# Batch 0's second softmax turned in 32x32 squares on VectorE, first group first, and the router's matrix in four column tiles

## The chip, the cores and the metric

The kernel runs on one core of one Trainium2 chip. The metric is the device time of one execution in microseconds (us). Before the change it is 726.91 us, the median of three runs (722.82 to 727.24). The engines are TensorE (PE in the rows; its weight loads are PEld), VectorE (DVE), ScalarE (ACT), GpSimd (POOL) and SyncE (SP), and each works through its own queue in order.

## The reference, cut to what matters

There are 8 batches, 8 heads, 576 positions, head dimension 64, 32 packing vectors per head, and a model width of 512.

```python
def sm_attn(qq, kk, vv):                       # softmax of scale * q k^T, times v
    ...
p_packed = sm_attn(p, k, v)                    # first softmax: 32 x 576 per head
out = sm_attn(q, p_packed, p_packed)           # second softmax: 576 x 32 per head
...
gate_pre += conv_w[k] * xp[:, k:k + S, :]      # causal convolution, 5 taps
gate = 1.0 / (1.0 + np.exp(-gate_pre))
val = x @ w_val
x2 = gate * val @ w_out
...
logits = x2 @ w_gate ; local_gate = sigmoid(x2 @ w_local)   # chooses an expert per position
out[b, s] = p[e] * (np.maximum(x2[b, s] @ w1[e], 0.0) @ w2[e])
```

The weights w_val, conv_w and w_out are stored as 64-bit floats and converted on the chip.

## The kernel before

For each batch the kernel computes, in this order: scores of packing vectors against keys (`s1`), first softmax (`softmax1`), its transposes (`a1T`), packed values `pp` (`a1v`), their transpose ppT, scores of queries against them (`s2`, tile s2k), second softmax, the packed values times w_val (`mval`, tile mv), attention output with the convolution (tile xT), `val` times the gate, `logits` and `route`, and the product with w_out (`x2`). Then `expert` runs the two layers of the expert that the first position chose; this is the bulk of the work. Heads are held in two groups g of four heads; the convolution's result has four blocks m of 128 channels, two in each group.

A planner (`Plan.run`) writes out every engine's order before the launch. Each task has an estimated duration, the tasks that must precede it, and tiles in numbered slots. At each step the planner takes the engine that can start first, and of its tasks that can start within 30 ns of the first one, the task with the lowest rank. A rank is the due time, counted back from the expert's goals, plus `later`. The conversion of w_out has `later` 30000. `behind` lets a task start only after another one has started. The estimate for `a1v` is 40 * STEPV + 250 ns. Only the order is kept: on the chip an engine waits for whatever its next instruction needs. PSUM has three slots of two banks for everything but the expert (tag p) and two single banks for the expert (tag f).

Around the change, batch 0 differs from the later batches. Its second softmax (`softmax2_0`, L447) copies the scores to SBUF, turns them on TensorE (L456), runs the softmax on VectorE over both groups (L467 to L477), and turns them back on TensorE (`a2T`, L518). The later batches (`softmax2`, L479) turn them in 32x32 squares on VectorE (L491 and L503), without TensorE. For the convolution, batch 0 forms on TensorE the five taps spread out as matrices (`taps`, L581), multiplies them into `pp` on VectorE (L593, L596), and then does five shifted products for each output block on TensorE (`conv0`, L610). The later batches do one product (`xT`, L552), scale the last tap on ScalarE (L560), add the other four on VectorE straight from PSUM (L564), and take the tanh on ScalarE (L567). The products of batch 0 are in 32-bit floats; each gives two records in the trace. The later ones split their operands into a high and a low half (`split`, L309: the high half on ScalarE, L312, the low one on VectorE, L316) and take three products (`mm3`, L298).

`router` (L666) computes w_out times the router's weights g9 (512 x 9): it turns w_out on TensorE (L677), copies it (L681), and takes 16 products with w_out stationary and 9 moving columns (L688). `logits` (L705) uses the result ww, and `x2` (L656) follows. `setup` loads the weights and converts them (`from_f64`, L897). The loads of the setup come from the SP queue, apart from some small ones; the loads of later batches come from the POOL queue.

Of the kernel before, what the change touches and what calls it, by code (L numbers as in the profile page):

```python
# [13 lines left out]
ALU = mybir.AluOpType  # L14
# [164 lines left out]

PERIOD, MARGIN, SLACK, START, DMA = 87000, 1e6, 1200, 75000, 3500  # L180
EARLY, LATE = 30, 30000
STEP8, STEPV = 30, 27
A2F = 1
TAPS, WARM, RATE, S1B = 'a1v', True, 415.0, [(0, 'xT', 1)]
LASTX = 30000
NPF, NPP, NPS = 2, 3, 0
ACC, WLO, F64 = 4, "POOL", "DVE DVE"
# [4 lines left out]
def packed_attention_gated_conv_moe(  # L192
# [238 lines left out]
    def s2(b):  # L431

        t, qt = st[b, "ppT"], [st[b, "q", j] for j in range(2)]
        pk = [pst([128, 2, 512], f"s2k_{b}_{g}") for g in range(2)]

        def prod():
            for hf in range(2):
                for i, g in heads():
                    n = slice(i % 2 * S + hf * HS, i % 2 * S + hf * HS + HS)
                    nc.tensor.matmul(pk[g][col(i), hf, 0:HS], t[row(g), col(i)], qt[i // 2][row(g), n],  # L440
                                     start=True, stop=True)

        st[b, "s2"] = pe(STEP8 * 32 + 250, prod, r=[t, *qt], w=pk, behind=done((b - 1, "a2T")))
        for g in range(2):
            (softmax2 if b else softmax2_0)(b, g, pk[g])

    def softmax2_0(b, g, pk):  # L447

        sT = ref(big, [128, 640], F32, f"a2l{g}", f"s2t_{g}", 1)
        act(S, lambda: cp(two(sT[:, 0:S]), halves(pk), AF.Copy), ps=True, r=[pk], w=[(sT, 0)])  # L450
        dve(64, lambda: nc.vector.memset(sT[:, S:], 0.0), w=[(sT, 1)])
        ps = pst([128, 8, 128], f"s2_{b}_{g}")

        def turn():
            for c in range(NT):
                nc.tensor.transpose(ps[:, c, :], sT[:, c * 128:c * 128 + 128], ident)  # L456

        pe(5 * 109, turn, r=[sT, f["ident"]], w=[ps])
        r = ref(sm, [128, 3, 20], F32, "s2r", f"s2r_{b}_{g}", 2)
# [7 lines left out]
        dve(640, lambda: nc.vector.tensor_reduce(r[:, 0, :], pv(), AX.X, ALU.max), r=[ps], w=[r])  # L467
        dve(640, lambda: tt(av(), pv(), bc(0), ALU.subtract), r=[ps, r], w=[a2])
        act(640, lambda: cp(a2[:], a2[:], AF.Exp, scale=0.125), r=[a2], w=[a2])
        dve(640, lambda: nc.vector.tensor_reduce(r[:, 1, :], av(), AX.X, ALU.add), r=[a2], w=[r])  # L470
# [5 lines left out]
        dve(280, end, sb=2, r=[r], w=[r])  # L476
        dve(700, lambda: tt(av(), av(), bc(2), ALU.mult), sb=2, r=[a2, r], w=[a2])  # L477

    def softmax2(b, g, pk):  # L479


        nj = S // NP
        a2 = ref(wk, [128, NT * 128], F32, "a2", f"a2_{b}_{g}", 2)
        a2f = st[b, "a2T", g] = ref(wk, [128, S], F32, "a2f", f"a2f_{b}_{g}", A2F)
        r = ref(sm, [128, 3, 20], F32, "s2r", f"s2r_{b}_{g}", 2)
        av = lambda: a2.t[:, 0:S].rearrange("p (j k) -> p j k", k=NP)

        def bc(i):
            return r[:, i, 0:nj].unsqueeze(2).to_broadcast([128, nj, NP])

        dve(S, lambda: nc.vector.transpose(two(a2[:, 0:S]), halves(pk)), r=[pk], w=[a2])  # L491
        dve(S, lambda: nc.vector.tensor_reduce(r[:, 0, 0:nj], av(), AX.X, ALU.max), r=[a2], w=[r])
        dve(S, lambda: tt(av(), av(), bc(0), ALU.subtract), sb=2, r=[r], w=[a2])
        act(S, lambda: cp(a2[:, 0:S], a2[:, 0:S], AF.Exp, scale=0.125), r=[a2], w=[a2])
        dve(S, lambda: nc.vector.tensor_reduce(r[:, 1, 0:nj], av(), AX.X, ALU.add), r=[a2], w=[r])
# [5 lines left out]
        dve(280, end, sb=2, r=[r], w=[r])  # L501
        dve(S, lambda: tt(av(), av(), bc(2), ALU.mult), sb=2, r=[r], w=[a2])
        dve(S, lambda: nc.vector.transpose(a2f[:], a2[:, 0:S]), r=[a2], w=[a2f])  # L503

    def a2T(b, g):
        if b:
            t = st[b, "a2T", g]
            hi = ref(big, [128, S], F32R, f"a2h{g}", f"a2h{g}_{b}", 1)
            lo = ref(big, [128, S], F32R, f"a2l{g}", f"a2l{g}_{b}", 1)
            split(S, lambda: hi[:], lambda: lo[:], lambda: t[:], [t], [hi, lo])  # L510
            st[b, "a2T", g] = (hi, lo)
            return
        a2 = st[b, "a2", g]
        ps = pst([128, 1024], f"a2Tp_{b}_{g}")

# [20 lines left out]
    def xT(b, g):  # L536


        pp, a2 = st[b, "pp", g][b > 0:], st[b, "a2T", g]
        terms = [(0, 0), (0, 1), (1, 0)] if b else [(0, 0)]  # L540
        pss_ = [pst([128, 1024], f"xT_{b}_{2 * g + i}") for i in range(2)]

        def x(i):
            return pss_[i][:, 512 - HS:512 + HS]

        def prod():
            for hf in range(2):
                n = slice(hf * HS, hf * HS + HS)
                for t, (wi, xi) in enumerate(terms):
                    for i in range(2):  # L550
                        m = slice(i * 64, i * 64 + 64)
                        nc.tensor.matmul(x(i)[:, n], pp[wi][m, :], a2[xi][m, n],  # L552
                                         start=(t == 0), stop=(t == len(terms) - 1))

        st["xT"] = st[b, "xT", g] = pe(mm(6) + 200 if b else 1500, prod, r=[*pp, *a2], w=pss_,
                                       behind=done((b - 1, "val"), "val0") if g == 0 else done((b, "val")))
        for i in range(2):
            j, ps = 2 * g + i, pss_[i]
            acc = st[b, "t", j] = ref(wk, [128, S], F32, "acc", f"acc_{b}_{j}", ACC)
            act(S + 100, lambda i=i, j=j, acc=acc: cp(acc[:], x(i), AF.Copy, scale=cw[:, j, KC - 1:KC]),  # L560
                ps=True, r=[ps, f["cw"]], w=[acc])
            for k in range(KC - 1):
                d = KC - 1 - k
                dve(S + 60, lambda i=i, j=j, k=k, d=d, acc=acc: stt(  # L564
                    acc[:, d:], x(i)[:, 0:S - d], cw[:, j, k:k + 1], acc[:, d:], ALU.mult, ALU.add),
                    r=[ps], w=[acc])
            act(S, lambda acc=acc: cp(acc[:], acc[:], AF.Tanh, scale=0.5), r=[acc], w=[acc])  # L567

    def taps():
# [5 lines left out]
            return ps[:, c * 128:c * 128 + 128]  # L575

        def prod():
            for g in range(2):
                for k in range(KC):
                    for i in range(2):  # L580
                        nc.tensor.matmul(place(g, k)[i * 64:i * 64 + 64],  # L581
                                         cw[:, 2 * g + i, k:k + 1].to_broadcast([128, 64]), ident,
                                         start=True, stop=True)

        pe(40 * 60, prod, r=[f["cw"], f["ident"]], w=st["taps"], behind=done(TAPS))

    def conv0(g):

# [77 lines left out]
    def router():  # L666
# [3 lines left out]
        for h in range(2):  # L670
            ps = pst([128, 1024], f"woT{h}")

            def turn(h=h, ps=ps):
# [6 lines left out]
            pe(8 * 109, turn, r=[wo, f["ident"]], w=[ps])  # L680
            act(1024, lambda h=h, ps=ps: cp(woT[:, h * 1024:h * 1024 + 1024], ps[:], AF.Copy), ps=True,  # L681
                r=[ps], w=[(woT, h)])
        ps = pst([128, 1024], "wwp")

        def prod():
# [234 lines left out]
    def setup():  # L920
# [4 lines left out]
        v64 = ref(big, [128, 8 * S], I32, "hh", "val64", 1)  # L925
        o64 = ref(big, [128, 8 * S], I32, "hl", "out64", 1)
        g9 = st["g9"] = ref(sm, [128, 4, 9], F32, "g9", "g9", 1)

        def half(t, src, k):
            q = nc.sync  # L930
# [5 lines left out]
        for x in SETUP.split():  # L936
# [10 lines left out]
            elif x[0] == "w":  # L947
                half(v64 if x[1] == "v" else o64, w_val if x[1] == "v" else w_out, int(x[2]))
            else:
                load(0, x[0], int(x[1]) if x[1:] else 0, nc.sync)  # L950

        def flat(t, k):
            return t.rearrange("p k c -> p (k c)")[:, k * CH:(k + 1) * CH]
# [25 lines left out]
    def attention(b):  # L979
# [9 lines left out]
            a1v(b, g)  # L989
        ppT(b)  # L990
        mval(b)
        if not b:
            taps()
        for g in range(2):
            if b:
                load(b, "q", g, nc.gpsimd)
        s2(b)
        for g in range(2):
            a2T(b, g)
        for g in range(2):  # L1000
            if b:
# [164 lines left out]
```

## Time and profile before

| what | before |
|---|---|
| median of three runs | 726.91 us |
| the profiled execution | 727.72 us |
| its span, first to last instruction | 726.0 us |
| mean granted TensorE clock | 0.977 of 2.4 GHz |
| TensorE busy | 687.0 us, 95% of the span |
| VectorE busy | 430.7 us, 59% |
| ScalarE busy | 289.8 us, 40% |
| GpSimd busy | 236.1 us, 33% |

The span lies inside the execution's own time; the difference of 1.7 us is before the first and after the last instruction. Busy time says how much work an engine has, not where it is waited for. The chain of waits says that: it follows the last instruction back through whatever released it. A "x40" behind a piece counts records.

### The profile page before, as it was taken

What the parts mean: (1) busy time and instruction counts of PE and PEld (TensorE: products, weight loads), DVE (VectorE), ACT (ScalarE), POOL (GpSimd) and SP (SyncE); (2) the same over time, 40 slices, a digit from 0 to 9 for tenths busy, and PEclk for the clock granted to TensorE, in tenths of its full rate; (3) what the DMA queues carried; (4) which work ended last, traced back from release to release, by engine and by line L of the source; (5) the groups of instructions that cost most, each with busy time, mean ns of one, the idle gap of its engine ahead of it and who ended that gap; (6) DMA issues with size and microseconds to landing.
All of it is one profiled execution on the core that took longest, in us unless ns stands there. A gap on an engine that the chain in (4) does not pass through costs nothing.

```text
span 726.0 us, 15236 instructions
## 1 busy us (share of the span) xinstructions
PE 687.0 (95%) x6124; PEld 640.6 (88%) x6124; DVE 430.7 (59%) x874; ACT 289.8 (40%) x565; POOL 236.1 (33%) x250
## 2 busy tenths in 40 slices
PE   3589999999899989999999999999999999999996
PEld 2367989997899879899989989999999999999996
DVE  5972358845884697958688578627972663221311
ACT  3533345433552346444446245424353333312420
POOL 2020344224320623413353044412342144325441
PEclk9877999999899999999999999999999999999999
DMA  8601394228421943715482356314242335243322
GB/s 348 242 1 32 127 330 143 77 85 266 171 60 48 310 153 120 233 49 184 150 257 80 131 183 222 90 45 176 82 134 74 131 97 153 83 165 127 111 89 67
DMA packets 35293, 102.10 MB, mean 141 GB/s; under 512 B 4283, under 2 KB 6899, under 8 KB 32659
## 3 DMA queue, kind: packets, MB, share of 16 engines
q0 software_dynamic: 13616, 56.87, 22.3%
q1 hardware_dynamic: 21314, 44.00, 19.6%
q8 instruction: 50, 0.82, 0.5%
q10 hardware_dynamic: 288, 0.21, 0.1%
q14 instruction: 25, 0.20, 0.1%
HBM read 74.90 MB, written 28.52 MB: 142 GB/s over the span
## 4 chain that ended last, share of the span: by engine, by line
PE 81%; DMA 8%; DVE 4%; issue 3%; POOL 1%; ACT 1%; SPq 0%; POOLq 0%; DVEq 0%; ACTq 0%
PE g L299 17%; PE g L301 16%; PE g L300 15%; DMA codes<-rk 5%; PE x L299 5%; PE x L300 5%; PE x L301 5%; PE val L299 2%; PE val L300 2%; PE val L301 2%; DMA out<-in_w_out_dram 2%; PE xT L552 2%; PE xT L610 2%; PE lg L705 1%; DVE codes L815 1%
## 5 line engine op out<-in xcount | busy, mean ns | idle before, releaser
L314 POOL TENSOR_TENSOR wlo<-raw,whi 128x512 fp32r<-128x512 f32 x128 | 166.4, 1301 | 281.3 <-ACT whi L312 279.0
L299 PE MATMUL g<-x2h,whi 128*128 128x288 f32 x512 | 154.5, 302 | 3.9 <-DVE hl L866 3.8
L299 PE MATMUL g<-hh,whi 128*128 128x288 f32 x512 | 154.2, 301 | 0.4 <-ACT whi L312 0.4
L301 PE MATMUL g<-hh,wlo 128*128 128x288 f32 x512 | 150.9, 295 | 0.9 <-POOL wlo L314 0.9
L301 PE MATMUL g<-x2h,wlo 128*128 128x288 f32 x512 | 151.5, 296 | 0.0
L300 PE MATMUL g<-x2l,whi 128*128 128x288 f32 x512 | 151.5, 296 | 0.0
L300 PE MATMUL g<-hl,whi 128*128 128x288 f32 x512 | 150.7, 294 | 0.0
L312 ACT ACTIVATE whi<-raw 128x512 fp32r<-128x512 f32 x128 | 80.2, 627 | 95.3 <-PE g L300 55.1
L299 PEld LDWEIGHTS g<-x2h,whi 128*128 128x128 f32 x512 | 96.7, 189 | 10.2 <-DVE hl L866 5.3
L299 PEld LDWEIGHTS g<-hh,whi 128*128 128x128 f32 x512 | 96.1, 188 | 7.0 <-issue 5.7
L866 DVE SCALAR_TENSOR_TENSOR hl<-g,hh 128x288 fp32r<-128x288 f32 x128 | 57.7, 453 | 74.9 <-ACT hh L864 74.1
L864 ACT ACTIVATE hh<-g 128x288 fp32r<-128x288 f32 x128 | 52.5, 410 | 114.0 <-PE g L301 113.2
L301 PEld LDWEIGHTS g<-hh,wlo 128*128 128x128 f32 x512 | 96.0, 188 | 1.1 <-POOL wlo L314 1.1
L300 PEld LDWEIGHTS g<-x2l,whi 128*128 128x128 f32 x512 | 96.8, 189 | 0.0
L301 PEld LDWEIGHTS g<-x2h,wlo 128*128 128x128 f32 x512 | 96.7, 189 | 0.0
L300 PEld LDWEIGHTS g<-hl,whi 128*128 128x128 f32 x512 | 96.1, 188 | 0.0
L564 DVE SCALAR_TENSOR_TENSOR acc<-xT,cw,acc 128x572 f32<-128x572 f32 (+3 forms) x112 | 85.0, 806 | 6.7 <-ACT acc L560 6.7
L299 PE MATMUL x<-gh,wout_hi 128*128 128x288 f32 x256 | 76.9, 300 | 0.8 <-ACT ltT L710 0.8
L300 PE MATMUL x<-gl,wout_hi 128*128 128x288 f32 x256 | 76.2, 298 | 0.0
L301 PE MATMUL x<-gh,wout_lo 128*128 128x288 f32 x256 | 75.9, 296 | 0.0
L884 DVE TENSOR_TENSOR y<-g,rows 128x288 f32<-128x288 f32 x64 | 28.9, 452 | 60.1 <-PE g L301 60.1
L662 DVE SCALAR_TENSOR_TENSOR x2l<-x,x2h 128x576 fp32r<-128x576 f32 x32 | 24.2, 756 | 62.7 <-ACT x2h L661 62.7
(174 smaller groups left out, 1058.4 us busy)
## 6 DMA issues: line engine op xcount, KB each, us to landing
raw<-in_wE_dram SPq DMA_DIRECT2D x128, 256.0 KB, 2.7
xs<-x2h POOLq DMA_DIRECT2D x8, 1152.0 KB, 4.6
xs<-x2l POOLq DMA_DIRECT2D x8, 1152.0 KB, 6.9
v<-in_v_dram POOLq DMA_DIRECT2D x14, 640.0 KB, 5.9
out_dram<-y POOLq DMA_DIRECT2D x31, 288.0 KB, 3.2
k<-in_kT_dram POOLq DMA_DIRECT2D x14, 576.0 KB, 4.8
q<-in_qT_dram POOLq DMA_DIRECT2D x14, 576.0 KB, 6.2
rows<-rk SPq DMA_DIRECT2D x8, 288.0 KB, 3.9
```

Of the source, the lines that this page charges most:

```text
L299: nc.tensor.matmul(o, lhi, rhi, start=start, stop=False)
L300: nc.tensor.matmul(o, lhi, rlo, start=False, stop=False)
L301: nc.tensor.matmul(o, llo, rhi, start=False, stop=stop)
L312: t = act(n, lambda: cp(hi(), src(), AF.Copy), ps=ps, r=r, w=[h], behind=behind)
L314: pool(n, lambda: nc.gpsimd.tensor_tensor(lo(), src(), f32(hi()), ALU.subtract), r=[*r, h], w=[l])
L552: nc.tensor.matmul(x(i)[:, n], pp[wi][m, :], a2[xi][m, n], start=(t == 0), stop=(t == len(terms) - 1))
L564: dve(S + 60, lambda i=i, j=j, k=k, d=d, acc=acc: stt(acc[:, d:], x(i)[:, 0:S - d], cw[:, j, k:k + 1], acc[:, d:], ALU.mult, ALU.add), r=[ ...
L610: nc.tensor.matmul(x(i)[:, lo:hi], w[m], a2[m, lo - d:hi - d], start=(k == KC - 1), stop=(k == 0))
L662: dve(S, lambda: stt(two(xlo[:, m, :]), halves(ps), 0.5, f32(two(xhi[:, m, :])), ALU.mult, ALU.subtract), r=[ps, (xhi, m)], w=[(xlo, m)])
L864: act(HS, lambda ps=ps, u=u, n=n: cp(hh[:, u, n], ps[:, 0:HS], AF.Relu), ps=True, r=[ps], w=[(hh, (u, hf))], goal=goal, urgent=True)
L866: dve(HS, lambda ps=ps, u=u, n=n: stt(hl[:, u, n], ps[:, 0:HS], 0.0, f32(hh[:, u, n]), ALU.max, ALU.subtract), r=[ps, (hh, (u, hf))], w=[( ...
L884: dve(HS, lambda ps=ps, hf=hf, n=n, y=y: tt(y[:, n], ps[hf][:, 0:HS], st[b, "w"][:, n], ALU.mult), r=[ps[hf], st[b, "w"]], w=[(y, hf)], go ...
```

## The change

Batch 0 takes `softmax2` like the others, with group 1's VectorE tasks ranked 3000 later (`late`, G0). Its `a2T` becomes the plain 32-bit result of the last transpose, and two buffers of a2f exist instead of one (A2F). `taps` and `conv0` stay for both groups of batch 0: the lines that test CONV1 are there, but CONV1 is False, so they change nothing, nor does the new index of `pp` in `xT`. The taps are computed behind batch 0's `s2` instead of behind `a1v`. The router's matrix is computed with the padded weights g9p (32 columns) stationary, one quarter of the inner dimension in each of four column tiles, and w_out's turned copy moving 512 columns; the result is copied, turned back in four transposes, and its four parts are added by one reduction on VectorE. STEPV goes from 27 to 14 for all batches.

```diff
-STEP8, STEPV = 30, 27
-A2F = 1
-TAPS, WARM, RATE, S1B = 'a1v', True, 415.0, [(0, 'xT', 1)]
+STEP8, STEPV = 30, 14
+WWCOL, CONV1, G0, TURN0 = True, False, 3000, True
+A2F = 2
+TAPS, WARM, RATE, S1B = (0, 's2'), True, 415.0, [(0, 'xT', 1)]
...
         for g in range(2):
-            (softmax2 if b else softmax2_0)(b, g, pk[g])
+            (softmax2 if b or TURN0 else softmax2_0)(b, g, pk[g])
...
     def softmax2(b, g, pk):
         nj = S // NP
+        late = 0 if b else G0 * g
...
-        dve(S, lambda: nc.vector.transpose(two(a2[:, 0:S]), halves(pk)), r=[pk], w=[a2])
+        dve(S, lambda: nc.vector.transpose(two(a2[:, 0:S]), halves(pk)), r=[pk], w=[a2], later=late)
...
     def a2T(b, g):
+        if TURN0 and not b:
+            st[b, "a2T", g] = (st[b, "a2T", g],)
+            return
...
-        pe(40 * 60, prod, r=[f["cw"], f["ident"]], w=st["taps"], behind=done(TAPS))
+        pe((20 if CONV1 else 40) * 60, prod, r=[f["cw"], f["ident"]], w=st["taps"], behind=done(TAPS))
...
+        if WWCOL:
+
+            gp = st["g9p"]
+            ps = pst([128, 1024], "wwq")
+
+            def prod():
+                for d in range(4):
+                    nc.tensor.matmul(ps[32 * d:32 * d + 32, 0:512], gp[:, d, :], woT[:, d * 512:d * 512 + 512],
+                                     start=True, stop=True)
+
+            pe(1100, prod, r=[woT, gp], w=[ps])
+            q = ref(big, [128, 8 * S], F32, "hl", "wwT", 1)
+            act(512, lambda: cp(q[:, 0:512], ps[:, 0:512], AF.Copy), ps=True, r=[ps], w=[q])
+            ps2 = pst([128, 1024], "wwp")
+
+            def back():
+                for k in range(4):
+                    nc.tensor.transpose(ps2[:, k * 128:k * 128 + 128], q[:, k * 128:k * 128 + 128], ident)
+
+            pe(4 * 109, back, r=[q, f["ident"]], w=[ps2])
+            dve(512, lambda: nc.vector.tensor_reduce(
+                ww[:, :, 0:9], ps2[:, 0:512].rearrange("p (k d e) -> p k e d", k=4, d=4)[:, :, 0:9, :],
+                AX.X, ALU.add), r=[ps2], w=[f["ww"]])
+            return
...
+        if WWCOL:
+            dve(128, lambda: nc.vector.memset(g9p[:], 0.0), w=[g9p])
+            dve(36, lambda: nc.vector.tensor_copy(g9p[:, :, 0:9], g9[:]), sb=2, r=[g9], w=[g9p], later=20000)
...
-        if not b:
-            taps()
...
         s2(b)
+        if not b:
+            taps()
```

## Rows read from the trace of the kernel before

**Rows 1.** The page's totals: busy us (share of the span) xinstructions.
```profile
PE 687.0 (95%) x6124; PEld 640.6 (88%) x6124; DVE 430.7 (59%) x874; ACT 289.8 (40%) x565; POOL 236.1 (33%) x250
```
**Rows 2.** The chain of waits, 0 to 76 us: start us, us, what.
```profile
11.35 14.62 DMA out<-in_w_out_dram
25.99 1.14 ACT wo L903
...
27.34 1.98 PE s2k L440 x32
29.32 1.71 PE mv L530 x16
...
40.79 6.99 PE xT L610 x40
47.77 4.08 PE val L635 x16
51.85 5.04 PE xT L610 x40
...
62.67 4.22 PE wwp L688 x32
...
69.00 2.12 PE lg L705 x16
...
71.84 0.61 PE x L299
```
**Rows 3.** Timeline of TensorE, 0 to 60 us: start us, us, instruction [idle before].
```profile
21.12 3.90 PE L581 MATMUL taps<-ident,cw 128*64 128x128 f32 x40
...
38.42 2.37 PE L518 MATMUL a2Tp<-ident,a 128*128 128x128 f32 x10 [6.13 <-DVE a L477]
...
56.82 1.97 PE L677 MATMUL woT<-ident,wo 128*128 128x128 f32 x16
```
**Rows 4.** Timeline of VectorE, 0 to 75 us.
```profile
31.78 1.56 DVE L467 TENSOR_REDUCE s2r<-s 128x20 f32<-128x640 f32 x2 [0.55 <-PE s L456]
...
34.72 0.69 DVE L906 TENSOR_SCALAR val<-out 128x1024 int32<-128x1024 int32 x1
...
37.51 1.49 DVE L477 TENSOR_TENSOR a<-a,s2r 128x640 f32<-128x640 f32 x2
...
41.91 4.51 DVE L915 TENSOR_TENSOR wo<-wo,val 128x1024 f32<-128x1024 f32 x2
46.46 1.23 DVE L916 SCALAR_TENSOR_TENSOR wo<-gt,wo 128x1024 f32<-128x1024 f32 x1
```
**Rows 5.** VectorE by line and shape: xcount | busy us, mean ns | idle before.
```profile
L493 DVE TENSOR_TENSOR a<-a,s2r 128x576 f32<-128x576 f32 x14 | 10.9, 785 | 0.0
...
L492 DVE TENSOR_REDUCE s2r<-a 128x18 f32<-128x576 f32 x14 | 9.8, 721 | 0.0
...
L498 DVE TENSOR_SCALAR s2r<-s2r 128x18 f32<-128x18 f32 x14 | 3.7, 262 | 0.0
...
L593 DVE TENSOR_TENSOR taps_a<-taps,ppf 128x512 f32<-128x512 f32 x2 | 1.4, 684 | 0.0
...
L596 DVE TENSOR_TENSOR taps_b<-taps,ppf 128x128 f32<-128x128 f32 x2 | 0.5, 281 | 0.0
```
**Rows 6.** ScalarE by line and shape: the later batches' exponential.
```profile
L494 ACT ACTIVATE a<-a 128x576 f32<-128x576 f32 x14 | 9.5, 683 | 11.1 <-DVE a L493 10.9
```
**Rows 7.** Windows: us, busy (x) of each engine, PEclk, DMA share, GB/s.
```profile
31.00:33.00 2.00, 1.29 (x13) 1.05 (x10) 1.45 (x3) 1.08 (x2) 0.00 (x0) 0.99 0.90 353
39.00:44.00 5.00, 5.00 (x23) 3.83 (x23) 4.93 (x6) 2.25 (x3) 1.50 (x1) 0.50 0.01 3
66.00:75.00 9.00, 8.23 (x66) 5.20 (x66) 2.25 (x8) 2.30 (x6) 1.62 (x3) 0.50 0.40 138
190.00:198.00 8.00, 6.38 (x30) 5.88 (x31) 5.59 (x12) 5.92 (x12) 2.56 (x2) 0.59 0.24 67
```
**Rows 8.** The chain of waits, later: logits at full speed.
```profile
149.46 1.11 PE lg L705 x16
```

More of the change, by code (lines that the diff above doesn't have):

```diff
@@ L458, in softmax2_0 @@
         pe(5 * 109, turn, r=[sT, f["ident"]], w=[ps])
+        late = G0 * g
         r = ref(sm, [128, 3, 20], F32, "s2r", f"s2r_{b}_{g}", 2)
@@ L465, in bc @@
             return r[:, i, :].unsqueeze(2).to_broadcast([128, 20, NP])
-        dve(640, lambda: nc.vector.tensor_reduce(r[:, 0, :], pv(), AX.X, ALU.max), r=[ps], w=[r])
-        dve(640, lambda: tt(av(), pv(), bc(0), ALU.subtract), r=[ps, r], w=[a2])
+        dve(640, lambda: nc.vector.tensor_reduce(r[:, 0, :], pv(), AX.X, ALU.max), r=[ps], w=[r], later=late)
+        dve(640, lambda: tt(av(), pv(), bc(0), ALU.subtract), r=[ps, r], w=[a2], later=late)
         act(640, lambda: cp(a2[:], a2[:], AF.Exp, scale=0.125), r=[a2], w=[a2])
-        dve(640, lambda: nc.vector.tensor_reduce(r[:, 1, :], av(), AX.X, ALU.add), r=[a2], w=[r])
+        dve(640, lambda: nc.vector.tensor_reduce(r[:, 1, :], av(), AX.X, ALU.add), r=[a2], w=[r], later=late)
         def end():
@@ L474, in end @@
             nc.vector.reciprocal(r[:, 2, :], r[:, 1, :])
-        dve(280, end, sb=2, r=[r], w=[r])
-        dve(700, lambda: tt(av(), av(), bc(2), ALU.mult), sb=2, r=[a2, r], w=[a2])
+        dve(280, end, sb=2, r=[r], w=[r], later=late)
+        dve(700, lambda: tt(av(), av(), bc(2), ALU.mult), sb=2, r=[a2, r], w=[a2], later=late)
     def softmax2(b, g, pk):
         nj = S // NP
+        late = 0 if b else G0 * g
         a2 = ref(wk, [128, NT * 128], F32, "a2", f"a2_{b}_{g}", 2)
@@ L489, in bc @@
             return r[:, i, 0:nj].unsqueeze(2).to_broadcast([128, nj, NP])
-        dve(S, lambda: nc.vector.transpose(two(a2[:, 0:S]), halves(pk)), r=[pk], w=[a2])
-        dve(S, lambda: nc.vector.tensor_reduce(r[:, 0, 0:nj], av(), AX.X, ALU.max), r=[a2], w=[r])
-        dve(S, lambda: tt(av(), av(), bc(0), ALU.subtract), sb=2, r=[r], w=[a2])
+        dve(S, lambda: nc.vector.transpose(two(a2[:, 0:S]), halves(pk)), r=[pk], w=[a2], later=late)
+        dve(S, lambda: nc.vector.tensor_reduce(r[:, 0, 0:nj], av(), AX.X, ALU.max), r=[a2], w=[r], later=late)
+        dve(S, lambda: tt(av(), av(), bc(0), ALU.subtract), sb=2, r=[r], w=[a2], later=late)
         act(S, lambda: cp(a2[:, 0:S], a2[:, 0:S], AF.Exp, scale=0.125), r=[a2], w=[a2])
-        dve(S, lambda: nc.vector.tensor_reduce(r[:, 1, 0:nj], av(), AX.X, ALU.add), r=[a2], w=[r])
+        dve(S, lambda: nc.vector.tensor_reduce(r[:, 1, 0:nj], av(), AX.X, ALU.add), r=[a2], w=[r], later=late)
         def end():
@@ L499, in end @@
             nc.vector.reciprocal(r[:, 2, 0:nj], r[:, 1, 0:nj])
-        dve(280, end, sb=2, r=[r], w=[r])
-        dve(S, lambda: tt(av(), av(), bc(2), ALU.mult), sb=2, r=[r], w=[a2])
-        dve(S, lambda: nc.vector.transpose(a2f[:], a2[:, 0:S]), r=[a2], w=[a2f])
+        dve(280, end, sb=2, r=[r], w=[r], later=late)
+        dve(S, lambda: tt(av(), av(), bc(2), ALU.mult), sb=2, r=[r], w=[a2], later=late)
+        dve(S, lambda: nc.vector.transpose(a2f[:], a2[:, 0:S]), r=[a2], w=[a2f], later=late)
     def a2T(b, g):
+        if TURN0 and not b:
+            st[b, "a2T", g] = (st[b, "a2T", g],)
+            return
         if b:
@@ L536, in xT @@
     def xT(b, g):
-        pp, a2 = st[b, "pp", g][b > 0:], st[b, "a2T", g]
+        pp, a2 = st[b, "pp", g][-2:], st[b, "a2T", g]
         terms = [(0, 0), (0, 1), (1, 0)] if b else [(0, 0)]
@@ L577, in prod @@
         def prod():
-            for g in range(2):
+            for g in range(1 if CONV1 else 2):
                 for k in range(KC):
@@ L927, in setup @@
         g9 = st["g9"] = ref(sm, [128, 4, 9], F32, "g9", "g9", 1)
+        g9p = st["g9p"] = ref(sm, [128, 4, 32], F32, "g9p", "g9p", 1)
         def half(t, src, k):
@@ L1000, in attention @@
         for g in range(2):
-            if b:
+            if b or g and CONV1:
                 xT(b, g)
```

## The prediction

> **What bounds the kernel now.** I read the engine totals first: TensorE is busy for 687.0 of 726.0 us [rows 1], so the end moves with the work that TensorE has to do, the level of its clock, and the time in which it has nothing to do. Then I read the chain of waits through the start [rows 2], because all but two constants of the change lie in batch 0. From 71.84 us, the first product of `x2(0)`, the chain stays on TensorE nearly without a break; so what the change does is, to first order, how far it moves those 71.84 us. Ahead of them the chain goes: a ScalarE conversion that waits for the second half of w_out (landed at 25.99), scores (27.34), second softmax, convolution of group 0 (40.79), `val` 0 and 1, convolution of group 1 (51.85), router (62.67), logits (69.00). TensorE's own timeline shows 6.13 us of idle ahead of the turn back at 38.42 [rows 3], which VectorE's softmax ends. VectorE's timeline prices that softmax [rows 4]; the grouped lines price the operations that batch 0 takes over from the later batches [rows 5, 6]; the windows show the clock [rows 7].
>
> The profiled execution took 727.72 us, 0.8 us above the median of 726.91. I subtract from it and carry the 0.8 over.
>
> **In front of the scores: nothing.** The taps (40 records, 3.90 us [rows 3]) leave the place in front of ppT. But the copy of ppT sits on ScalarE behind the conversion that starts at 25.99, when its data has landed [rows 2]. While that order stays, the scores start at 27.34 as before. The planner will think ppT ready earlier (shorter estimate for `pp`, no taps in front), so the order may turn; that is a rival.
>
> **The second softmax.** Before, the scores end at 29.32 and the first convolution product starts at 40.79: 11.5 us. Two copies and a turn on TensorE come first; VectorE takes from 31.78 to 39.00 for both groups in step [rows 4]; then come the turn back (2.37 us [rows 3]) and a copy. Now group 0 by itself is six passes of 0.721 to 0.785 us (4.5), two small ones of 0.26 (0.5) [rows 5] and an exponential of 0.683 [rows 6]: 5.7. On top come its tap products (0.684 + 0.281) and about 0.5 for a pass of other work that is running when it becomes ready. 29.3 + 7.2 = 36.5. The ends are 35.1 (the 5.7 alone) and 39 (a conversion pass, two passes of group 1 and group 1's tap products come between). I take 36.5, since group 1 ranks 3000 later and the conversions 30000. Gain here: 4.3.
>
> **The taps in their new place.** After `mval`, at 31.03, TensorE has nothing until 36.5. The taps fill 3.90 us of that at the granted clock of 31 to 33, 0.99 [rows 7]: hidden, ending at 34.9. At the 1.2 GHz level they would take 7.8, end at 38.8 and, with the products, hold the convolution until 39.8: 3.3 us. They hold one PSUM slot, free once the first transposes have read the scores, and one of the expert's two banks, which no expert needs yet.
>
> **The clock of the convolution.** Before, TensorE was idle from 32.3 to 38.4, its clock stood at 0.50, the 1.2 GHz level, from 39 to 44 [rows 7], and group 0's convolution took 6.99 us where group 1's like 40 records took 5.04 [rows 2]. Now the idle gap is 34.9 to 36.5. I take it that the clock stays up: 36.5 + 5.04 = 41.5. If it falls all the same, the convolution loses 2 to 3 us.
>
> **Group 1, `val`, the second convolution.** `val` 0 needs both groups. Behind group 0's last pass VectorE has of group 1 about four passes, the small ones, the exponential, and its tap products: 3.0 + 0.5 + 0.7 + 1.0 = 5.2, from about 36 to 41.2, so just in time. From 41.5 TensorE runs `val` 0 and 1 (4.08) to 45.6, the second convolution (5.04) to 50.6, the turn of w_out (1.97) to 52.6, and `val` 2 and 3 (as 0 and 1) to 56.7. This work is unchanged.
>
> **What is late next: w_out's conversion.** It ranks last on VectorE. The seven passes that stood between 34.72 and 46.46 sum to 9.6 us, with two of them slowed to 4.51 together [rows 4]. From about 29.6 VectorE does two softmaxes (9.4, an estimate: twice 5.0, less what neighbouring passes overlap), tap products 1.9, conversions 9.6: 20.9, to 50.5. The turn of w_out stands at 50.6. Any gating pass of `val` 0 and 1 put in front delays it by another pass (some 0.75 for 576 columns [rows 5]): up to 2 us of cover are missing. GpSimd's wout_lo follows and is needed only by `x2`.
>
> **The router.** 32 records in 4.22 us [rows 2] become four products into column tiles, a copy, four transposes and a reduction. The logits are of like shape: two rounds of four column tiles with 288 columns took 1.11 us [rows 8], so one round with 512 columns costs about 1.0; the transposes 0.5 (a quarter of 1.97); the copy 0.65 and the reduction 0.65 (0.683 and 0.721 are for 576 columns). TensorE gives up 4.22 us for 1.5, but the logits wait for the whole of it, 2.8 and some hops, 3.1: `s1(1)` (1 to 2 us) fits into the copy and the reduction. From 56.7: 59.8, logits at 60. The Trainium skill (TensorEngine Tiling (Array Packing), PSUM Bottleneck) warns that tiling speeds the array and not the emptying of PSUM; by it this edit is worth not 2.7 us but about 1.1, and the sum above agrees.
>
> **Logits to `x2`.** 2.84 us before, at 0.50 from 66 to 75 [rows 7]; 1.8 at full speed, with the logits at 1.11. I take 1.8: `x2` starts at 61.8, against 71.84: 10.0 us. `x2` itself began at the low level; full speed there would give 1.3 more, a low stretch elsewhere takes as much; I take 0.
>
> **The rest: nothing.** STEPV reaches every later batch through the planner's order, and A2F gives softmax a second buffer there. No row of before shows that other order. The nearest price is the worst stretch of the later batches, 190 to 198: 1.6 us idle and a clock of 0.59 [rows 7], together some 5 us. One such stall can go or come: −5 to +5, taken as 0. No DMA is added, and no step is moved past one on POOL or SP. Clearing and filling the padded g9 is two short VectorE passes in setup.
>
> Sum: 727.7 − 10.0 = 717.7 as profiled, 716.9 on the median; I say **717 us**.
>
> **Rivals.**
> - Holes: group 1 or w_out comes late, or the taps run at the low level; each costs 2 to 3 us of TensorE at once, and the clock can fall with it. Gain 5, 722. For it: both covers above are within a microsecond. Against: VectorE has had 4.93 busy of 5.00 us from 39 to 44 [rows 7] and can only be misordered, not starved. 0.19.
> - ppT goes ahead of the conversion: scores 3 us earlier, 714. For it: the conversions rank 30000 later. Against: they did so before, and one still stood in front [rows 2]. 0.10.
> - The later batches reorder: the stall of 190 to 198 goes, 712, 0.10; or one more comes, 722, 0.11. For both: the durations that the planner is given change in every batch.
> - The other side: TensorE sits at 1.2 GHz. From 36.5 to `x2` it has at full speed 5.0 + 4.1 + 5.0 + 2.0 + 4.1 + 1.5 + 1.1 + 1.1 = 23.9 us; every microsecond of it that runs low costs one more. Once more than 10 of the 23.9 run low, the change loses: at 18 low, 735. For it: in 66 to 75 the clock was 0.50 while TensorE was busy for 8.23 of 9 us, on small tiles [rows 7], and small tiles now run from 27 to 35. The Trainium skill (TensorE: Matmul & The Clock Gate, What's actually happening) has the throttled level as the default that activity lifts; by it the idle time taken out speaks for a higher clock, 715 to 717, and small tiles are not told apart. Against the rival: 0.99 from 31 to 33, behind scores and `mval` of such tiles. 0.06.
> - The groups finish together as before, because the planner's gaps never let group 0 go ahead: convolution at 39, gain 7; within the forecast's lower half.
>
> **Chances.** The forecast (714 to 720) has 0.44, the rest as given. A measurement here can tell a difference of 1%, 7.3 us, so 719.6 is the line. Below it lie the early ppT, the lost stall and nine tenths of the forecast: faster by over 1% 0.60. The holes, the added stall and the rest lie within 1%: 0.35. Slower by over 1% takes most of the low clock, 0.05. Range 709 to 724: from `x2` at 59 with the stall gone (717 − 3 − 5) to a start that gains 8 and a stall (719 + 5).
>
> **What would show it.** Right: first convolution product near 36.5, the convolution at 5 us, `x2` at 62, router records under 1.6 us together, later idle time as before. Wrong: ppT copied before 25.99; a gap over 1 us on TensorE between 41 and 60; a clock of 0.50 between 31 and 60; a new stall behind 90 us.

## The result, and the profile after

In the first series the changed kernel took **716.0 us** (median of 4 runs, 714.39 to 718.8) against 724.87 for the kernel before (4 runs): ratio **0.9868**, 95% interval 0.9823 to 0.9913. A later series of the same kernel gave 721.56 us (12 runs, 718.82 to 725.29) against 724.89: ratio 0.9963, 0.9939 to 0.9986. The two intervals don't meet. The change is faster, by 1.3% in the one series and 0.4% in the other; the forecast of 717 lies by the first median, and the second is 4.6 us above it.

The profiled execution of the first series took 718.8 us with a span of 717.1, so 8.9 us of span are gone. The page's totals come first (columns as in [rows 1]), with the granted clock in 40 slices:

```profile
PE 676.6 (94%) x6084; PEld 632.1 (88%) x6084; DVE 434.6 (61%) x879; ACT 287.4 (40%) x561; POOL 236.4 (33%) x250
...
PEclk9989999999899999999999999999999999999998
```

TensorE is busy for 10.4 us less and idle for 40.5 us (before: 39.0): products and their time at a low clock went, not idle time. The chain of waits through the start, which answers to [rows 2] (start us, us, what):

```profile
27.16 2.17 PE s2k L441 x32
29.34 2.90 PE taps L587 x40
32.23 1.10 PE mv L536 x16
33.36 1.08 ACT mh L417 x2
34.45 0.58 ACT a L497
...
35.05 0.75 DVE s2r L498
...
38.62 7.85 PE xT L616 x40
...
61.41 1.13 PE s L351 x32
62.54 1.04 PE wwq L696 x8
63.60 0.61 ACT wwT L701
64.25 0.40 PE x L300
66.11 0.44 PE wwp L706 x4
...
69.72 1.11 PE lg L735 x16
```

The reader is to see three things. The first convolution starts 2.1 us earlier than before (38.62 against 40.72 on the timeline), but takes 7.85 us, longer than the 6.99 of before [rows 2]. So `val` 3 ends at 61.41, only 1.3 us earlier than before (62.67). And `x2(0)` starts 2.84 us behind that, where it started 9.17 us behind it before: it no longer stands behind the logits, which now come inside it, at 69.72. TensorE's timeline and the windows show the gap and the clock around the first convolution; the last window answers to the third of [rows 7]:

```profile
38.62 1.42 PE L616 MATMUL xT<-a2f,taps_b 64*128 64x288 f32 x4 [5.37 <-DVE a2f L506]
```
```profile
35.00:37.00 2.00, 0.00 (x0) 0.00 (x0) 1.92 (x6) 0.59 (x2) 0.00 (x0) 1.00 0.00 0
37.00:39.00 2.00, 0.38 (x2) 0.41 (x4) 2.00 (x4) 0.00 (x0) 0.00 (x0) 0.57 0.00 0
39.00:41.00 2.00, 2.00 (x10) 1.90 (x10) 1.97 (x5) 0.00 (x0) 0.00 (x0) 0.50 0.04 8
...
66.00:75.00 9.00, 9.00 (x77) 8.15 (x76) 2.30 (x7) 2.35 (x5) 0.00 (x0) 1.00 0.20 79
```

TensorE stands idle for 5.37 us, the clock falls to the 1.2 GHz level ahead of the convolution and comes back only when most of it is done (0.72 from 43 to 45 us). From 66 to 75 us, at 0.50 before [rows 7], it is now 1.00. VectorE's timeline (start us, us, instruction, [idle before]) shows what stands ahead of group 0's last pass (`a2f`), which ends the wait:

```profile
29.45 1.45 DVE L494 STREAM_TRANSPOSE a<-s2k 128x576 f32<-128x576 f32 x2 [0.41 <-PE s2k L441]
30.83 1.37 DVE L495 TENSOR_REDUCE s2r<-a 128x18 f32<-128x576 f32 x2
32.11 0.75 DVE L496 TENSOR_TENSOR a<-a,s2r 128x576 f32<-128x576 f32 x1
32.78 0.69 DVE L599 TENSOR_TENSOR taps_a<-taps,ppf 128x512 f32<-128x512 f32 x1
33.38 0.75 DVE L496 TENSOR_TENSOR a<-a,s2r 128x576 f32<-128x576 f32 x1
35.05 0.75 DVE L498 TENSOR_REDUCE s2r<-a 128x18 f32<-128x576 f32 x1 [0.92 <-ACT a L497]
35.72 0.68 DVE L599 TENSOR_TENSOR taps_a<-taps,ppf 128x512 f32<-128x512 f32 x1
...
37.71 0.77 DVE L506 STREAM_TRANSPOSE a2f<-a 128x576 f32<-128x576 f32 x1
```

The passes appear twice: group 1's transpose, maximum, subtraction and tap products (about 2.9 us) stand between group 0's, and so does a wait of 0.92 us for the exponential. The exponential (34.45 in the chain) stands on ScalarE behind the two copies of `mh`; these wait for `mval`, and `mval` stands on TensorE behind the taps. The rank of 3000 did not keep group 1 behind.

Behind 87 us the granted clock and TensorE's waits (7.1 us in all, before 9.5) are of the same size as before, but in other places. The longest new stall, on VectorE's timeline and then on TensorE's:

```profile
176.75 1.36 DVE L845 TENSOR_TENSOR_SCAN codes<-codes 128x576 bf16<-128x576 bf16 x1 [3.78 <-DMA codes<-rk]
178.03 0.80 DVE L896 SCALAR_TENSOR_TENSOR hl<-g,hh 128x288 fp32r<-128x288 f32 x2
```
```profile
178.51 0.61 PE L300 MATMUL g<-x2h,whi 128*128 128x288 f32 x1 [3.57 <-DVE hl L896]
```

The scan waits 3.78 us for its DMA. Behind it in VectorE's order stands `hl`, which reads an expert result g out of PSUM, and the next product into g waits 3.57 us for that; before, the longest such wait was 0.8. The Trainium skill (TensorE: Matmul & The Clock Gate, Architectural detail: the array is 16× 32×32, not 1× 128×128) calls VectorE's and ScalarE's queues strictly first in, first out; the rows agree. Over all batches the scans waited 11.5 us (7 times), before 7.3 (8 times).

### The profile page after: what moved, and what is told of

It reads as the page before. It is cut to its first block, busy times and chain, and to the rows that moved or that the text cites. A ratio compares the mean times of both kernels' runs of the same rounds, so it can differ in the third digit from the quotient of the medians.

```text
span 717.1 us, 15168 instructions
## 1 busy us (share of the span) xinstructions
PE 676.6 (94%) x6084; PEld 632.1 (88%) x6084; DVE 434.6 (61%) x879; ACT 287.4 (40%) x561; POOL 236.4 (33%) x250
## 4 chain that ended last, share of the span: by engine, by line
PE 82%; DMA 8%; issue 5%; POOL 2%; DVE 2%; ACT 1%; SPq 0%; POOLq 0%; DVEq 0%
PE g L300 17%; PE g L302 16%; PE g L301 16%; PE x L300 5%; PE x L301 5%; PE x L302 5%; DMA codes<-rk 4%; PE val L300 2%; PE val L301 2%; PE val L302 2%; DMA out<-in_w_out_dram 2%; PE xT L616 2%; PE xT L558 2%; POOL wlo L315 2%; PE pp L392 1%
## 5 line engine op out<-in xcount | busy, mean ns | idle before, releaser
L313 ACT ACTIVATE whi<-raw 128x512 fp32r<-128x512 f32 x128 | 80.3, 628 | 106.0 <-PE g L301 57.0
```

Source lines behind the costliest of these rows:

```text
L313: t = act(n, lambda: cp(hi(), src(), AF.Copy), ps=ps, r=r, w=[h], behind=behind)
```

## The experiments

Each kernel is compared with the kernel before in the same series. The ratios rest on 4 to 12 executions of each kernel; the other columns come from one profiled execution each. The table puts these side by side, all times from TensorE's timelines in us: from the first score product to the first convolution product, the first convolution, the end of `val` 3, the first product of expert(0), the stretch from there to the last batch's logits, and the ratio with its interval. From those logits to the end it was 139.1 to 142.5 everywhere.

| kernel | scores to conv. | conv. 0 | val 3 ends | expert(0) | expert(0) to last logits | ratio |
|---|---|---|---|---|---|---|
| before | 13.4 | 7.0 | 62.7 | 87.7 | 497.7 | |
| after | 11.5 | 7.8 | 61.4 | 80.8 | 496.0 | 0.9868 (0.9823–0.9913) |
| after, again | 12.4 | 6.6 | 60.9 | 80.3 | 498.6 | 0.9963 (0.9939–0.9986) |
| turn only | 12.8 | 6.8 | 60.8 | 83.0 | 499.1 | 1.0036 (1.0012–1.0060) |
| router only | 13.9 | 5.4 | 61.2 | 81.3 | 506.7 | 1.0059 (1.0034–1.0084) |
| STEPV 27 | 12.8 | 6.8 | 61.9 | 81.3 | 497.1 | 0.9902 (0.9868–0.9936) |
| mval first | 11.2 | 6.6 | 59.0 | 78.4 | 495.5 | 0.9915 (0.9881–0.9949) |
| before, codes later | 14.0 | 5.4 | 60.5 | 84.0 | 488.9 | 0.9820 (0.9785–0.9855) |
| after, codes later | 11.6 | 7.8 | 61.8 | 81.2 | 494.7 | 0.9924 (0.9897–0.9952) |
| mval first, codes later | 11.3 | 6.8 | 60.6 | 80.0 | 496.9 | 0.9904 (0.9866–0.9942) |
| STEPV 27, codes later | 11.7 | 7.9 | 61.7 | 81.1 | 497.0 | 0.9940 (0.9918–0.9962) |
| the same, one a2f | 11.7 | 7.9 | 61.9 | 81.3 | 493.0 | 0.9854 (0.9828–0.9879) |
| filler | 11.2 | 5.0 | 58.7 | 78.2 | 501.7 | 0.9947 (0.9926–0.9968) |
| group 1 held | 13.0 | 7.0 | 61.0 | 81.0 | 500.9 | 1.0020 (0.9998–1.0041) |

### The parts, one at a time

The changed kernel again:

> The changed kernel once more, as the yardstick for the runs beside it. Theory S (the gain lies in batch 0's start): ratio to before 0.985 to 0.990, first product of x2(0) at 64 us. Rival L (much of it is the later batches' new order): the same here; the runs beside it tell them apart.

721.56 us, slower than the ratio that both theories expected; `x2(0)` came at 63.74. Its trace has the same order of instructions, expert(0) 0.5 us earlier, and a wait that the first has in small. The waits of TensorE from 330 to 420 us (engine, line, waited for: us in total, times, longest), first of the changed kernel, then of its repeat:

```profile
PE g L300 <- DVE code L856: 0.8, 1, 0.8
```
```profile
PE g L300 <- DVE code L856: 3.0, 1, 3.0
```

In the repeat the scan ahead of `code` waited 2.45 us for its DMA and took 2.87 us itself, where it had waited 1.79 and taken 1.36. The same order, with transfers that land a little differently, so differs by a stall. The two profiled executions are only 2.0 us apart (718.8 and 720.78), and this wait covers that; the rest of the 5.6 us between the medians is in neither profile.

The softmax's turn alone, with STEPV at 27:

```diff
-STEP8, STEPV = 30, 14
-WWCOL, CONV1, G0, TURN0 = True, False, 3000, True
+STEP8, STEPV = 30, 27
+WWCOL, CONV1, G0, TURN0 = False, False, 3000, True
```

> Only the turned softmax with the taps behind the scores and two a2f buffers; the router as before, STEPV 27. Theory S: convolution at 38.6 as in the changed kernel, so 5 to 6 us of the 7.6 at x2(0) remain, ratio 0.989 to 0.994. If the router's part carried the gain, the ratio is above 0.996. Rival L: above 0.996 too, with x2(0) early and the time lost again later.

727.26 us. The router's matrix alone, with the rest as before:

```diff
-STEP8, STEPV = 30, 14
-WWCOL, CONV1, G0, TURN0 = True, False, 3000, True
-A2F = 2
-TAPS, WARM, RATE, S1B = (0, 's2'), True, 415.0, [(0, 'xT', 1)]
+STEP8, STEPV = 30, 27
+WWCOL, CONV1, G0, TURN0 = True, False, 0, False
+A2F = 1
+TAPS, WARM, RATE, S1B = 'a1v', True, 415.0, [(0, 'xT', 1)]
```

> Only the router in column tiles; batch 0's softmax, the taps, a2f and STEPV as before. Theory S: convolution at 40.8 as before, x2(0) 2 to 4 us earlier (2.7 of TensorE's time, and the clock that falls during the old router's small products may stay up), ratio 0.994 to 0.997. If the clock were nothing: 0.997. Rival L: 1.00.

729.35 us. Only STEPV back at 27:

```diff
-STEP8, STEPV = 30, 14
+STEP8, STEPV = 30, 27
```

> The changed kernel with STEPV back at 27: batch 0's order on TensorE stays, only later batches are ordered otherwise. Theory S: x2(0) at 64 as in the changed kernel and the ratio within 0.004 of its own. Rival L: x2(0) at 64 as well, but a ratio of 0.992 or more, the loss in new idle time behind 90 us.

718.13 us. Each part alone is a little slower than the kernel before (0.4% and 0.6%), though the softmax's turn starts expert(0) 4.7 us earlier and the router 6.5. Together (STEPV 27) they start it 6.4 us earlier: the gains don't add, and the end doesn't follow the start. For the two parts that is what rival L expected, the time lost again later. STEPV 27 (0.9902) lies below what rival L expected for it, and 3.4 us below the changed kernel's repeat. The router alone loses everything behind expert(0); its waits there on TensorE:

```profile
PE g L300 <- DVE hl L896: 9.4, 7, 3.9
PE xT L558 <- ACT a2h L313: 3.0, 2, 1.5
```

In the kernel before the same two waits were 3.8 and 2.7 us. The pair "turn only" and "STEPV 27" differs in the router alone. From the end of `val` 3 to expert(0) it was 22.2 us with the old router and 19.4 with the new one; before it was 25.05. So beside the other settings the router is worth 2.8 of the 5.65 us gained there. Yet the router alone needs 20.0 us for this stretch, 5.0 less than before. The two shares overlap: either edit by itself gives an order with `x2` ahead of the logits (`x2(0)` at 65.89 and logits at 68.67 in "turn only", 65.67 and 67.46 in "router only"), and how the 5.65 divide is not shown. The windows from 66 to 70 us show the clock, first "turn only", then "STEPV 27":

```profile
66.00:68.00 2.00, 2.00 (x10) 2.00 (x11) 0.64 (x4) 1.28 (x4) 0.00 (x0) 0.60 0.59 238
68.00:70.00 2.00, 2.00 (x20) 0.99 (x18) 0.00 (x0) 0.00 (x0) 0.00 (x0) 0.55 0.00 0
```
```profile
66.00:68.00 2.00, 2.00 (x18) 2.00 (x17) 0.84 (x5) 0.89 (x4) 0.00 (x0) 1.00 0.98 396
68.00:70.00 2.00, 2.00 (x17) 1.99 (x16) 0.58 (x1) 0.65 (x1) 0.00 (x0) 1.00 0.15 58
```

Behind the old router (3.68 us of products that move 9 columns) the clock falls to the 1.2 GHz level; behind the new one it stays at 1.00. TensorE counts as busy for 2.00 of 2.00 us in all four windows.

### What held the first convolution

`mval` ahead of the taps, so that the copies of `mh` are off ScalarE before the exponential:

```diff
-TAPS, WARM, RATE, S1B = (0, 's2'), True, 415.0, [(0, 'xT', 1)]
+TAPS, WARM, RATE, S1B = (0, 'mval'), True, 415.0, [(0, 'xT', 1)]
```

> The changed kernel with the taps tied behind mval instead of behind the scores; the order of the other instructions stays. Theory M (mh's two copies, released late because the taps run first, hold group 0's exponential on ScalarE for 1.5 us): mh copied by 32.5, exponential at 32.9, convolution at 37.0 to 37.3 instead of 38.6, x2(0) at 62 to 63. Rival V (VectorE's own passes set the time): convolution still at 38 or later. Whole time: 1 to 3 us less than the changed kernel's, ratio 0.992 to 0.995, if the later batches don't take it back.

The convolution starts at 37.36 and `x2(0)` at 61.83, close to what Theory M had; the time is 718.74 us (ratio 0.9915). The wait for the exponential is gone, and VectorE goes from its first transpose to group 0's last pass without a break. Of VectorE's timeline:

```profile
29.21 1.44 DVE L494 STREAM_TRANSPOSE a<-s2k 128x576 f32<-128x576 f32 x2
...
36.44 0.77 DVE L506 STREAM_TRANSPOSE a2f<-a 128x576 f32<-128x576 f32 x1
```

From VectorE's first transpose to the convolution it is 8.15 us instead of 9.17: the wait was worth 1.0. Counted from the scores only 0.3 of it shows (11.2 us instead of 11.5), since here VectorE began 3.0 us behind the scores' start, behind a conversion pass, where it had begun 2.3 behind it. The rest of the earlier convolution is that the scores themselves were earlier (26.19). With the wait gone, VectorE's own passes set the time.

The wait is longer where the taps take longer. In the repeat of the changed kernel they took 3.95 us instead of 2.97 (TensorE's timeline), and group 0's sum waited 1.62 us for the exponential instead of 0.92 (VectorE's):

```profile
28.95 3.95 PE L587 MATMUL taps<-ident,cw 128*64 128x128 f32 x40
```
```profile
35.71 0.75 DVE L498 TENSOR_REDUCE s2r<-a 128x18 f32<-128x576 f32 x1 [1.62 <-ACT a L497]
```

Seven kernels of the table have this order: the changed kernel and its repeat, "turn only", "STEPV 27", and the changed kernel with the codes later and its two variants without `mval` first. Their taps took 2.97 to 4.34 us at a granted clock of 1.00, and the first column of the table, 11.5 to 12.8 us, follows them: 2.97, 3.10, 3.19, 3.21, 3.95, 4.28 and 4.34 us of taps go with 11.46, 11.60, 11.68, 11.70, 12.44, 12.78 and 12.82. In all seven the convolution starts 5.36 or 5.37 us after `mval` has ended. So in this order the taps, `mval`, the copies of `mh` and the exponential are the path, and VectorE's passes alone are not.

Group 1's subtraction and tap products held behind group 0's last pass:

```diff
+        hold = [] if b else done("t2")
...
-        dve(S, lambda: tt(av(), av(), bc(0), ALU.subtract), sb=2, r=[r], w=[a2], later=late)
+        dve(S, lambda: tt(av(), av(), bc(0), ALU.subtract), sb=2, r=[r], w=[a2], later=late, behind=hold)
```

(and the same tie at `conv0`'s two products.)

> The changed kernel with group 1's subtraction and tap products (on VectorE) tied behind group 0's last transposing pass, so that group 0 goes ahead alone. Theory V (the convolution started 2 us later than forecast because VectorE did four passes of group 1 between group 0's own): from the start of the scores to the first convolution product 10.0 us instead of 11.46, less what w_out's conversion passes take of the gaps that come free (all of it, if three of them slip in); then val 0, which needs group 1, is late: TensorE waits 1 to 3 us at val 0 for VectorE, and x2(0) stays within 1 us of 64. Rival H (hops between engines, not VectorE's passes, set the 11.46): it stays within 0.3 us of 11.46. Both expect the total in 716 to 723.

Neither theory had the number: 13.0 us, longer than either, and 726.23 us. Of VectorE's timeline:

```profile
32.45 1.21 DVE L948 TENSOR_TENSOR wo<-wo,val 128x1024 f32<-128x1024 f32 x1
...
34.24 1.21 DVE L948 TENSOR_TENSOR wo<-wo,val 128x1024 f32<-128x1024 f32 x1
...
35.76 0.63 DVE L939 TENSOR_SCALAR val<-out 128x1024 int32<-128x1024 int32 x1
...
36.97 1.22 DVE L941 SCALAR_TENSOR_TENSOR val<-out,val 128x1024 int32<-128x1024 int32 x1
38.10 0.77 DVE L507 STREAM_TRANSPOSE a2f<-a 128x576 f32<-128x576 f32 x1
```

Into each gap between two of group 0's passes the planner put a pass of w_out's conversion, four of them, 4.3 us, where Theory V had reckoned with three. Nothing on VectorE waits here from its first transpose to group 0's last pass, so in this kernel it is VectorE's other passes that hold the convolution, whichever they are, and Rival H is out: a rank of 30000 does not keep a pass out of a gap. `val` 0 did not wait for group 1.

### The clock of the first convolution

36 more transposes of the identity behind `mval`, whose results nothing reads:

```diff
+            for i in range(4):
+                fp = ref(psf, [128, 512], F32, "f", f"fill{i}", NPF)
+
+                def fill(fp=fp):
+                    for c in range(9):
+                        nc.tensor.transpose(fp[:, c % 4 * 128:c % 4 * 128 + 128], ident, ident)
+
+                pe(9 * 109, fill, r=[f["ident"]], w=[fp], behind=done((0, "mval")))
```

> The changed kernel with 36 more transposes of the identity (128x128) behind mval, whose results nothing reads, so that TensorE has work in most of 33 to 37 us. Theory K (the first convolution took 7.85 us instead of 5.04 because TensorE stood idle ahead of it): the granted clock stays at 1.00 from 33 to 47, the convolution takes 5.0 to 5.5 us, x2(0) starts 2 to 3 us earlier (61 to 62), and the time falls by as much, 715.5 to 719.5 beside a changed kernel of 718 to 721.6, if the later batches keep their order. Rival W (the convolution is slow because something else holds its products: the copies of xT, or val waiting for group 1): it stays at 7 us or more at a clock of 1.00 and x2(0) at 64.

The convolution starts at the same time and takes 5.03 us. The windows, and the first product:

```profile
37.00:39.00 2.00, 1.64 (x13) 1.35 (x15) 2.00 (x4) 0.00 (x0) 0.00 (x0) 1.00 0.00 0
39.00:41.00 2.00, 2.00 (x20) 1.60 (x18) 1.97 (x5) 0.00 (x0) 0.00 (x0) 1.00 0.00 0
```
```profile
38.51 0.76 PE L616 MATMUL xT<-a2f,taps_b 64*128 64x288 f32 x4 [0.36 <-DVE a2f L506]
```

Theory K holds for the convolution: the idle gap is what cost 2.8 us, and `x2(0)` comes at 61.53, 2.7 us earlier. The Trainium skill (TensorE: Matmul & The Clock Gate, What's actually happening) has the low level as the default that activity lifts; these rows agree. But the time is 721.59 us, no better than the changed kernel's repeat (721.56): the stretch from expert(0) to the last logits is 5.7 us longer than in the first profile of the changed kernel, and 3.1 longer than in the repeat. The longest waits behind 87 us (in the first profile the same two were 4.6 and 0.8):

```profile
PE g L300 <- DVE hl L896: 5.7, 4, 3.8
PE g L300 <- DVE code L856: 3.0, 1, 3.0
```

### The later batches: the scan's place

The scan behind the DMA of the codes was put later in VectorE's order, by telling the planner that the DMA takes 6000 ns longer. In the kernel before, and in the changed kernel and its variant with `mval` first:

```diff
-        dma(nc.gpsimd, 300000, lambda: rows_dma(c[:], None, b, None), r=[(f["rk"], b)], w=[c])
+        dma(nc.gpsimd, 300000, lambda: rows_dma(c[:], None, b, None), lat=6000, r=[(f["rk"], b)], w=[c])
```

> The kernel before, with one number changed: the planner is told that codes arrive 6 us later than it thought, so it puts the scan later in VectorE's order. Theory C (VectorE standing on the codes transfer stalls TensorE in the later batches, in both kernels): its 7.3 us of waiting go below 3, ratio 0.992 to 0.996. Rival P (each re-planning shuffles the later stalls, with no one cause): waiting on codes goes, other waits come, ratio 0.998 to 1.006.

> The changed kernel with the same one number. Theory C: the 11.5 us of VectorE's waiting on codes go below 3, TensorE's idle time behind 90 us falls by 4 or more, ratio 0.982 to 0.990; against the kernel before with that number it is 0.988 to 0.991, which is the start's gain alone. Rival P: 0.992 or more.

> Both: mval ahead of the taps and the later codes. Theories M and C together: 0.979 to 0.988, below each of them alone. Rival P: between 0.990 and 0.998 with no regard to what it is made of.

All scans' waits are gone in all three. In the kernel before it gave 711.44 us, **the lowest median of all kernels here** (ratio 0.982 against the changed kernel's 0.9868 and 0.9963; the interval overlaps the first of these), without any of the change. The longest waits of TensorE behind 87 us in it:

```profile
PE g L299 <- DVE hl L866: 2.2, 2, 1.5
PE g L301 <- POOL wlo L314: 1.4, 2, 1.0
...
```

The gain, 13.3 us, is far above what Theory C had (0.992 to 0.996) and above the 7.3 us of waiting that went: in its profile 3.7 us of it lie ahead of expert(0), and 8.8 from there to the last logits. In the changed kernel (718.86) and its variant (718.09) the same edit shows no clear gain: the ratios, 0.9924 and 0.9904, are those that Rival P expected, and other waits came in place of the scans', the largest of them 2.4 us in all, for an exponential on ScalarE. So that VectorE stood on this DMA is shown, and that the wait goes; that the 711.44 come from it is not.

So the later batches' settings of the change were taken back too: first STEPV, then A2F (batch 0's second group keeps a buffer of its own).

```diff
-STEP8, STEPV = 30, 14
+STEP8, STEPV = 30, 27
...
-        a2f = st[b, "a2T", g] = ref(wk, [128, S], F32, "a2f", f"a2f_{b}_{g}", A2F)
+        a2f = st[b, "a2T", g] = ref(wk, [128, S], F32, "a2f" if b or not g else "a2f1", f"a2f_{b}_{g}", 1)
```

> The changed kernel with STEPV back at 27, and the scan that reads the codes moved later in VectorE's order (the codes DMA is given to the planner as 6000 ns longer). Theory L (what the change gives back, it gives back in the later batches, through the order that the planner makes of them): against the changed kernel with the codes alone (718.9) the STEPV term is worth what it was worth without the codes, 3.4 us (721.6 to 718.1): 715.5, ratio near 0.987, and the stretch from the first product of expert(0) to the last logits 491 to 493 us instead of 494.7. Rival A (the two settings don't add; the planner's order of each variant is a draw of its own): anywhere in 716 to 722, with waits that neither variant had. Both expect x2(0) to start at 63 to 65 us, as in the changed kernel.

> As the one before, and the later batches go back to one a2f buffer as well (batch 0's second group keeps a buffer of its own), so all settings of the later batches are those of the kernel before with the codes moved (711.4), and only batch 0 has the change. Theory L: the stretch from expert(0) to the last logits comes near that kernel's 488.9 us, and the start is the changed kernel's (expert(0) at 80 to 81 against 84.0): 489 to 491 + 80.5 + 139.5 + 1.7 = 711 less what the last stage varies, so 708 to 711, ratio 0.977 to 0.981, the fastest of all. Rival A: the planner draws another order although the settings are the same, since the start moves everything behind it: 713 to 719, with waits of 2 us or more behind 90 us that the kernel before with the codes moved doesn't have.

720.38 and 714.63 us. STEPV 27 was worth 3.4 us without the moved scan (against the repeat; against the first series nothing) and nothing with it (its interval overlaps that of "after, codes later"): rival A for that one. With a single a2f buffer in the later batches the kernel is 5.8 us faster: the two intervals don't meet, and 4.0 of it lie between expert(0) and the last logits. Whether the buffer does it or the order that was drawn with it is not shown. The last kernel differs from "before, codes later" in batch 0 alone. It starts expert(0) 2.7 us earlier and takes 4.1 us longer from there to the last logits; its ratio is no better, and its 714.63 lie in Rival A's range: with the same settings for the later batches, the stretch behind an earlier start came out longer.

## Why the prediction came out as it did

The direction was right, and so was the mechanism in the main: `x2(0)` and expert(0) come earlier, by 7.6 and 6.9 us of the 10.0. That the total of the first series was met (716.0 for 717) is partly luck: the start gained 3.1 us less than forecast, the stretches behind it gained 2.0 in that profile and lost 0.5 in the next, and the repeat missed by 4.6. By the prediction's own list, a clock of 0.50 between 31 and 60 and a new stall behind 90 us say that a step was wrong. Point by point:

- **In front of the scores: right.** 27.16 against 27.34, behind the same conversion.
- **The second softmax: wrong by 2.1 us.** The step that failed is "about 0.5 for a pass of other work that is running when it becomes ready", taken "since group 1 ranks 3000 later". About 2.9 us of other work stood between group 0's passes, and the exponential was waited for besides. By the kernel with `mval` first, the exponential's wait is 1.0 of the 2.1, and VectorE's other passes are the rest. The upper end, 39, named the passes, not the wait, and was nearly reached. That the rank leaves no gap free is shown by the kernel with group 1 held.
- **The taps: not hidden.** They were forecast behind `mval`, filling idle time with 3.90 us. They took 2.90 to 2.97 in the first profile, but stood ahead of `mval`, and so delayed the copies of `mh` and the exponential behind these. That order cost the 1.0 us just named; in the repeat, with 3.95 us of taps, the path from VectorE's first transpose was 10.15 us, 2.0 longer than with `mval` first.
- **The clock of the convolution: wrong by 2.8 us.** "I take it that the clock stays up" rested on a gap of 1.6 us; the gap was 5.37, and the filler shows that it is the gap. The prediction had the price, "the convolution loses 2 to 3 us", but left it out of the sum. The nearest rival is the one of the holes, in which work comes late and "the clock can fall with it"; there group 1 or w_out was to be late, and here it was group 0 itself.
- **`val`, the second convolution, w_out: right.** From `val` 0 to the end of `val` 3 it was 15.0 us (forecast 15.2), and TensorE did not wait for w_out's conversion, whose last pass (54.02, 1.21 us) ended 2.3 us ahead of the turn.
- **Router and logits: right in price, wrong in order.** `wwq` and `wwp` take 1.48 us (forecast 1.5), the logits 1.11. The sum had `x2` wait for the logits; it did not, and started 2.84 us behind `val` 3 instead of 5.1. The last 0.72 us ahead of it is a wait for the copy of `wwq` out of PSUM. The logits' products then lie inside `x2`, and expert(0)'s weights come later: TensorE waits 1.07 us for `wlo` at 82.40. Counted to expert(0) this stretch gained 5.65 us where the forecast had 4.0. Up to `val` 3 it gained 1.3 where the forecast had 6.0. The two errors, −4.7 and +1.6, make the 6.9.
- **The rest: the bounds were too narrow.** The prediction took ±5 for "one such stall can go or come". In the first profile the rest gained 2.0 us (8.9 − 6.9), in the repeat it lost 0.5 (726.0 − 719.1 = 6.9, of 7.4). Over all kernels the stretch from expert(0) to the last logits went from 488.9 to 506.7, where it was 497.7 before. So the term that the forecast set at 0 went from −8.8 to +9.0, nearly twice the bounds that it had been given, and as large as the gain at the start.

What stays open: why the planner put `x2` ahead of the logits, what makes the stretch behind expert(0) shorter or longer from order to order, why the same taps take 2.8 to 4.3 us behind the scores, and why two series of the changed kernel differ by 5.6 us while the medians of the kernel before beside all series lie at 723.7 to 724.9. One stall of 3.0 us is seen; the rest is not in these profiles.

## What to carry to other kernels

In a kernel whose order is computed from estimated durations, a gain at the start need not reach the end: compare matched points (here the first expert and the last logits), and price the new order behind it by a spread, not by one stall. Work moved into idle time is hidden only if nothing on the path stands behind it in its engine's order: here the taps delayed `mval`, and through it the softmax. An idle gap on TensorE costs its length and the low clock behind it (here 2.8 us), so ask of each edit where the next gap is. And look for the in-order engine that stands on a DMA: here a wait of 3.78 us on VectorE became one of 3.57 us on TensorE. But run the cure in more than one kernel: moving the scan went with 13.3 us less in the kernel before, and with no clear gain in the changed one.

## What the hardware showed that was not expected

- The clock fell during products of 9 moving columns while TensorE counted as busy throughout. Windows of the kernel before (the old router runs from 62.67 to 66.89):

```profile
62.00:64.00 2.00, 2.00 (x18) 1.87 (x16) 1.42 (x2) 0.45 (x2) 0.00 (x0) 1.00 0.00 0
64.00:66.00 2.00, 2.00 (x17) 2.00 (x16) 0.76 (x1) 0.54 (x1) 0.00 (x0) 0.80 0.01 4
66.00:68.00 2.00, 2.00 (x29) 1.46 (x36) 0.00 (x0) 0.21 (x1) 0.00 (x0) 0.50 0.00 0
```

  It fell behind the same router in "turn only" and in the kernel before with the codes later (to 0.55 and 0.50), and not in "router only", "STEPV 27" or the changed kernel, with the new one. The Trainium skill (TensorE: Matmul & The Clock Gate, What's actually happening) has the throttle released by activity; here the profile counts full busy time and the clock fell all the same, and the rows decide.
- After like gaps the clock comes back at different times: behind 5.37 us of idle the convolution took 7.8 us in the changed kernel, and behind 5.36 us 6.6 in its repeat. In the order of before it took 7.0 us in the kernel before and 5.4 with the codes moved. So 1.2 to 1.6 us between two starts in the table can be of this kind.
- The same 40 products of the taps took 2.8 to 4.3 us behind the scores, at a granted clock of 1.00 in every window from 27 to 33 us: of the changed kernel 2.97, of its repeat 3.95.
- The scan of the codes takes 1.36 us or up to 2.87 us, the same instruction on the same shape.
